# Squared-ReLU attention and two feed-forward layers on one core: the first layer's first token block placed beside the last attention block alone, with GpSimd splitting that block's squares

## The chip, the core and the metric

The kernel runs on one NeuronCore of a Trainium2 chip. The engines are named as in the profile: PE (TensorE, matrix products; PEld is its weight load), DVE (VectorE), ACT (ScalarE), POOL (GpSimd) and SP (SyncE, which only issues transfers here). The metric is the device time of one execution in microseconds; lower is better. Several runs give a median.

## What is computed

```python
def _attn_ref(u, v, z):                      # u, v: 2 x 3008 x 256, z: 2 x 3008 x 64
    scores = (1.0 / S) * np.matmul(z, z.transpose(0, 2, 1))
    attn = np.maximum(scores, 0.0) ** 2
    return (u * np.matmul(attn, v)).astype(np.float32)

def _moe_ref(x, w_in, w_out, a, b):          # x: 6016 x 256, d_ff = 2048
    h = x @ w_in
    P = a[0] + a[1] * h + a[2] * h**2 + a[3] * h**3
    Q = 1.0 + abs(b[0]) * abs(h) + abs(b[1]) * h**2
    return ((P / (Q + 1e-06)) @ w_out).astype(np.float32)

def _moe2_ref(x, w_in, w_out):
    h = x @ w_in
    return (np.maximum(0.01 * h, h) @ w_out).astype(np.float32)

reference = _moe2_ref(_moe_ref(_attn_ref(u, v, z).reshape(6016, 256), ...), ...)
```

## The kernel before

**Numbers in two parts.** Every factor of a product is split into a high part, rounded to fp32r, and a low part, the rest. A product takes three passes on PE: high by high, low by high, high by low. So each tile that ends on PE first needs a rounding (a copy or an activation with an fp32r output) and a subtraction.

**Attention.** Queries are cut into 12 blocks, six for each batch: 512 wide, the sixth (blocks 5 and 11) 448 wide. A block meets 24 key blocks of 128 rows, two at a time, so it has 12 steps (`NPAIR`), numbered through as `t` from 0 to 143 (`NT`). A step is: the scores on PE (`scores_pe`), ReLU and square on ACT (`scores_relu`, `scores_square`), the square's high part and low part on DVE (`square_high`, line 337, and `square_low`, line 343; at some steps ACT writes the high part instead, set `by_act`, line 289), and two steps later the product with V on PE (`av`, line 350). The tiles `r` have three slots, `ph` three, `pl` two.

**Two forms of a block.** Blocks below `SPLIT` (line 84, 10 of them) use 64-row pairs. A score has 64 rows of contraction, so two matmuls of 64 rows stand side by side in the array: six half matmuls a step. In `av` each 128-row product is two half products into two accumulators, 24 a step; at the block's end ACT copies one accumulator (`copy_half`), DVE adds the other (`add_half`) and multiplies by `u` (`gate_halves`). Blocks from `SPLIT` on use 128 rows: the keys' high and low parts are stacked by `stack_keys`, through DRAM, in the steps around `FULL = SPLIT * NPAIR`; a score is four full matmuls, `av` twelve, and `gate` multiplies straight from the accumulators. The other two accumulator banks are then free for `y1`.

**First feed-forward layer.** The 6016 tokens are cut into 12 blocks of 512 (the last 384), the hidden width into eight chunks (`NP`) of 256. Chunk `c` takes: `m1_h`, 12 matmuls into an `h` tile; on ACT `m1_tb`, `m1_s`, `m1_v` (three readings of `h`); on DVE `m1_q` and the two operations of `m1_w`; on ACT `m1_r` (logarithm, then exponential: the reciprocal); on DVE `m1_gh`, `m1_back` and the two of `m1_gl`; then `m1_y`, 12 matmuls into `y1`. Of the seven DVE operations the two of `m1_w` read `h` in PSUM and one tile in SBUF; the other five read two tiles in SBUF. `h` and the score tiles share two PSUM tiles (`big`), used in turn.

**The order of the work** is the order in which the program calls these functions: every engine runs its own list in that order and waits for tiles. From step `m0 = NT + DEPTH - 3 * MERGED` = 119 to the last step, chunks 0 to 8 (`MERGED = NP + 1`) are laid between the steps, one for every three steps:

```python
    m0 = NT + DEPTH - 3 * MERGED
    for t in range(NT + DEPTH):
        c, ph = divmod(t - m0, 3)
```

So the first token block's layer runs beside the last two attention blocks, 10 and 11. Chunk 9's `h` follows at step 144. From chunk 9 on the main loop (lines 853 to 892) pairs each chunk of the first layer with one of the second layer eight chunks back. `tasks`, filled by `at(step, f)`, holds the transfers and small jobs of a step: loads of `u`, of `x1` (`load_x`, `split_x1`), the second layer's weights (`load_w2`), the stores of `xs`. All transfers go through SP, but for a few on ACT at the start and the end.

Of the kernel before, what the change touches and what calls it, by code (L numbers as in the profile page):

```python
# [9 lines left out]
F32 = mybir.dt.float32  # L10
# [7 lines left out]
def f32(ap):  # L18
    return ap.bitcast(F32)
# [3 lines left out]
def squared_relu_attention_moe_moe2(  # L23
# [57 lines left out]

    HALVES = slice(0, 64), slice(64, P)

    SPLIT = NB - 2

    def key_block(i, pr, e):
        if i >= SPLIT or blocks[i][0] == 0 and pr < 4:
# [198 lines left out]
    R, PH, PL = {}, {}, {}  # L286

    SC = {}
    by_act = {0, 1, 2, SPLIT * NPAIR + 2, SPLIT * NPAIR + 3, NB * NPAIR - 2, NB * NPAIR - 1}

    def scores_pe(t):
        i, pr = divmod(t, NPAIR)
# [40 lines left out]

    def scores_square(t):
        act.activation(R[t], R[t], AF.Square)  # L335

    def square_high(t):
        if t in by_act:
# [11 lines left out]
    def av(t, part=None):  # L350
        i, pr = divmod(t, NPAIR)
        b, q0, n = blocks[i]
        ph, pl = PH[t], PL.get(t)
        if part != 0:
            PH.pop(t), PL.pop(t)
        seq = [(0, ph), (1, ph), (0, pl)]
        if i < SPLIT:
            if pr == 0 and part != 1:
                pacc[i] = [acc(k, f"oT{i}_{k}") for k in range(2)]
            steps = [(si, e, j) for si in range(3) for e in range(2) for j in range(2)]  # L360
            if pr == NPAIR - 1:
                steps.sort(key=lambda x: (x[2], (x[:2] == (2, 1)) != x[2]))
            elif pr == 0:
                steps.sort(key=lambda x: x[2] if i else x[0] == 2)
            ops = [(si, e, j, r) for si, e, j in steps for r in range(2)
                   if key_block(i, pr, e) < KB - 1 or si == 1 or si == 2 and r == j]
            last = {(j, r): k for k, (_, _, j, r) in enumerate(ops)}
            for k, (si, e, j, r) in enumerate(ops):
                if part is not None and part != (e == 1 or si == 2):
                    continue  # L370
                h, mv = seq[si]
                kb, rows = key_block(i, pr, e), HALVES[r]
                o = (kb % 4) * D + j * P
                pe.matmul(pacc[i][r][j][:, :n], V[b, kb // 4][rows, h, o : o + P], mv[rows, e, :],  # L374
                          start=pr == 0 and si == 0 and e == 0, stop=pr == NPAIR - 1 and last[j, r] == k)
            if pr == NPAIR - 1:
                at(t + DEPTH + 2, lambda: sp.dma_start(xs[i], uT.pop(i)[:, :, :n]))
            return
        if pr == 0:
            pacc[i] = acc(own_acc(i), f"oT{i}")  # L380
        a = pacc[i]
        for si, (h, mv) in enumerate(seq):
            for e in range(2):
                kb = 2 * pr + e
                if kb == KB - 1 and si == 0:
# [239 lines left out]
    def m1_h(c):  # L625
        i, p = divmod(c, NP)
        T[c] = {"n": tokens[i][1], "h": hidden(f"h1_{c}", 0, p, X1[i], tokens[i][1])}

    def m1_tile(c, key, k, dt=F32):
        T[c][key] = slot(k, f"{key}_{c}", dt)[:, :, : T[c]["n"]]  # L630
        return T[c][key]

    def m1_tb(c):
        if c % 2 and c <= MERGED:
            T[c]["t1"] = extra[1][:, :, : T[c]["n"]]
        else:
            m1_tile(c, "t1", 13 if c % 2 else 2)
        act.activation(T[c]["t1"], T[c]["h"], AF.Abs, scale=b0)  # L638

    def m1_s(c):  # L640
        act.activation(m1_tile(c, "t2", 11 if c == NP else 7 if c > NP and c % 2 else 3), T[c]["h"], AF.Square)  # L641

    def m1_v(c):
        act.activation(m1_tile(c, "t3", 12 if c % 2 else 10), T[c]["h"], AF.Identity, scale=ca[3], bias=ca[2])  # L644
# [98 lines left out]

    TAIL = NC - NP
    MERGED = NP + 1
    m0 = NT + DEPTH - 3 * MERGED
    at(m0 - 5, lambda: load_x(0))
    at(m0 - 3, lambda: split_x1(0))
    at(m0 - 2, lambda: split_x1_low(0))
# [5 lines left out]
    at(20, lambda: act.activation(par[:, 6:7], par[:, 5:6], AF.Abs))  # L755
    for f in tasks.pop(-1):
        f()
    for t in range(NT + DEPTH):
        c, ph = divmod(t - m0, 3)
        c = c if t >= m0 and c < MERGED else None  # L760
        ends = DEPTH < t < FULL and (t - DEPTH + 1) % NPAIR == 0
        waits = ends or DEPTH < t < FULL and (t - DEPTH + 2) % NPAIR == 0
        if t < NT and t != FULL + 1:
            if t == DEPTH:
                av(0, 0)
            if t:
                scores_pe(t)
            if not ends:
                scores_act(t)
            if c == 1 and ph == 2:  # L770
                m1_r(c)
                m1_gh(c)
                m1_back(c)
        if c is not None and ph == 0 and t != FULL - 1:
            m1_h(c)
        if c and c > 1 and ph == 1:
            m1_y(c - 1, (0, 1, 2))
        if t == NT:
            m1_h(MERGED)
        if t >= DEPTH and t != FULL + 1:  # L780
            av(t - DEPTH, 1 if t == DEPTH else None)
        if c == 1 and ph == 1:
            m1_y(0, (0, 1, 2))
        if t == FULL - 1:
            m1_h(c)
        if t == FULL:
            av(t - 1)
            scores_pe(t + 1)
            joined = copy_half(SPLIT - 1, 12)
            add_half(SPLIT - 1, joined)  # L790
            scores_relu(t + 1)
        if ends:
            i = (t - DEPTH) // NPAIR
            joined = copy_half(i, 9)
            scores_act(t)
            add_half(i, joined)
            for f in tasks.pop(t - 1, []):
                f()
        if c == 1 and ph == 0:
            m1_v(c)  # L800
            m1_tb(c)
            m1_s(c)
            m1_w(c)
        if t < NT:
            square_high(t)
        if t == FULL - 1:
            square_low(t)
        if c is not None and c != 1 and ph == 0:
            if c == 0:
                m1_v(c)  # L810
            m1_tb(c)
            m1_s(c)
            if c:
                m1_v(c)
            if c < NP:
                m1_w(c)
            m1_q(c)
        if t == 4:
            tasks[t].pop(0)()
        if t < NT and t != FULL - 1:  # L820
            square_low(t)
        if c == 1 and ph == 0:
            m1_q(c)
        if ends:
            tasks.setdefault(t + 1 + (t + 1 in conv4_at), []).insert(0, lambda i=i, o=joined: gate_halves(i, o))
        if t == FULL:
            gate_halves(SPLIT - 1, joined)
        if c == NP and ph == 0:
            m1_w(c)
        if ends or not waits:  # L830
            for f in tasks.pop(t, []):
                f()
        if c is not None and c != 1 and ph == 1:
            m1_r(c)
            if c == NP:
                split_x2_high(0)
            if c == 0:
                scores_square(FULL + 1)
            m1_gh(c)
            if c == NP:  # L840
                split_x2_low(0)
            m1_back(c)
        if t == NT + 1:
            m1_v(MERGED)
            m1_tb(MERGED)
            m1_s(MERGED)
            m1_w(MERGED)
            m1_q(MERGED)
        if c is not None and ph == 2:
            m1_gl(c)  # L850
    assert not tasks

    for c in range(MERGED, NC):
# [89 lines left out]
```

## Time and profile before

| | |
|---|---|
| median of 3 runs | 1518.52 us (1518.33 to 1521.3) |
| the profiled execution | 1518.12 us, of which its span is 1516.3 us |
| busy in the span | PE 1510.2 us (8546 matmuls), DVE 1346.7, ACT 1111.3, POOL 1.1 |
| granted TensorE clock | 0.9 or more in every slice, mean 1.0 |

The span is the time from the first to the last recorded instruction; the profiled execution's own time holds about 1.8 us around it. Matmuls are pipelined, so the busy time of PE says only that it had work in hand; how long a group of matmuls takes is read from the chain of waits, which follows the last instruction back to what released each step. A duration of an operation on DVE or ACT is a little longer than the distance from one start to the next, since neighbours overlap by some 0.1 us.

### The profile page before, as it was taken

The numbers are of one execution on the slowest core, as the hardware profiler recorded it, in microseconds if no ns is written. First come the engines' busy times: TensorE is split into PE (matmuls) and PEld (weight loads), VectorE is DVE, ScalarE is ACT, GpSimd is POOL, SyncE is SP. The second block draws the span as 40 slices with busy tenths as digits, with TensorE's granted clock in tenths as the row PEclk, the third lists the DMA queues.
The fourth block names the chain that finished last, engine by engine and source line by source line (L and its number), as shares of the span: only waits on it lengthen the run. The fifth ranks groups of instructions, "written<-read, shape, count | busy, mean of one in ns | idle before, by whom it ended". The sixth has DMA issues, their size and how long they took to land.

```text
span 1516.3 us, 21013 instructions
## 1 busy us (share of the span) xinstructions
PE 1510.2 (100%) x8546; PEld 1265.8 (83%) x8546; DVE 1346.7 (89%) x1315; ACT 1111.3 (73%) x1146; POOL 1.1 (0%) x9
## 2 busy tenths in 40 slices
PE   9999999999999999999999999999999999999998
PEld 7888888888788888888888888888888888888888
DVE  8888878888799999999999999999999999999872
ACT  8888878888777866777777676767676767676653
POOL 0000000000000000000000000000000000000000
PEclk9999999999999999999999999999999999999999
DMA  7433426354411520000000000100000000000001
GB/s 177 98 93 95 125 77 144 112 160 138 135 27 35 173 82 14 14 1 14 14 15 14 14 15 0 22 7 14 14 15 14 14 15 0 11 15 1 15 0 25
DMA packets 140351, 74.75 MB, mean 49 GB/s; under 512 B 114528, under 2 KB 124000, under 8 KB 139232
## 3 DMA queue, kind: packets, MB, share of 16 engines
q1 hardware_dynamic: 137584, 72.96, 18.9%
q8 instruction: 67, 1.10, 0.3%
q10 hardware_dynamic: 2672, 0.46, 0.2%
q14 instruction: 28, 0.23, 0.1%
HBM read 46.27 MB, written 21.50 MB: 45 GB/s over the span
## 4 chain that ended last, share of the span: by engine, by line
PE 100%; ACT 0%; DVE 0%; issue 0%
PE h L610 34%; PE y L621 34%; PE oT L374 21%; PE sc L301 5%; PE oT L390 4%; PE sc L308 1%; PE warm L194 0%; ACT r L323 0%; PE zT0q L166 0%; DVE yo L740 0%; ACT sq L210 0%; PE zT0b L166 0%; PE zT0k L166 0%; DVE wt L190 0%
## 5 line engine op out<-in xcount | busy, mean ns | idle before, releaser
L621 PE MATMUL y<-gh,w 128*128 128x512 f32 (+1 forms) x1536 | 373.3, 385 | 0.0
L621 PEld LDWEIGHTS y<-gh,w 128*128 128x128 f32 x1536 | 286.8, 188 | 54.3
L374 PE MATMUL oT<-ph,V 64*128 64x512 f32 (+1 forms) x1880 | 234.0, 384 | 0.0
L374 PEld LDWEIGHTS oT<-ph,V 64*128 64x128 f32 x1880 | 175.9, 184 | 35.5 <-issue 0.4
L621 PE MATMUL y<-gl,w 128*128 128x512 f32 (+1 forms) x768 | 202.2, 385 | 0.0
L638 ACT ACTIVATE t<-h,par 128x1024 f32<-128x1024 f32 (+1 forms) x91 | 100.2, 1101 | 130.4 <-PE h L610 130.4
L697 ACT ACTIVATE gh<-h 128x1024 fp32r<-128x1024 f32 (+1 forms) x96 | 97.0, 1011 | 134.2 <-PE y L621 111.2
L610 PE MATMUL h<-x2h,w 128*128 128x512 f32 (+1 forms) x768 | 186.5, 385 | 0.0
L621 PEld LDWEIGHTS y<-gl,w 128*128 128x128 f32 x768 | 143.5, 188 | 28.0
L610 PEld LDWEIGHTS h<-x2h,w 128*128 128x128 f32 x768 | 143.4, 188 | 27.2
L648 DVE SCALAR_TENSOR_TENSOR t<-t,par,t 128x1024 f32<-128x1024 f32 (+1 forms) x91 | 114.2, 1255 | 31.2 <-ACT t L641 31.2
L657 ACT ACTIVATE t<-t,par 128x1024 f32<-128x1024 f32 (+1 forms) x91 | 103.3, 1135 | 44.1 <-DVE t L648 44.1
L704 DVE TENSOR_TENSOR gl<-g,gh 128x1024 fp32r<-128x1024 f32 (+1 forms) x96 | 115.0, 1198 | 23.2 <-ACT g L699 23.2
L610 PE MATMUL h<-x,w 128*128 128x512 f32 (+1 forms) x576 | 133.5, 380 | 0.0
L374 PE MATMUL oT<-pl,V 64*128 64x512 f32 (+1 forms) x940 | 128.1, 384 | 0.0
L347 DVE TENSOR_TENSOR pl<-r,ph 128x1024 fp32r<-128x1024 f32 (+2 forms) x97 | 115.5, 1192 | 12.2 <-ACT r L335 4.2
L664 DVE SCALAR_TENSOR_TENSOR gh<-t,par,t 128x1024 fp32r<-128x1024 f32 (+1 forms) x91 | 114.6, 1260 | 10.6 <-ACT x2h L588 0.5
L672 DVE SCALAR_TENSOR_TENSOR t<-t,par,t 128x1024 f32<-128x1024 f32 (+1 forms) x96 | 121.1, 1261 | 3.1
L653 DVE SCALAR_TENSOR_TENSOR t<-t,par,h 128x1024 f32<-128x1024 f32 (+1 forms) x96 | 120.8, 1258 | 3.4
L610 PEld LDWEIGHTS h<-x,w 128*128 128x128 f32 x576 | 107.1, 188 | 19.6 <-issue 0.4
L652 DVE TENSOR_TENSOR t<-t,h 128x1024 f32<-128x1024 f32 (+1 forms) x96 | 114.4, 1192 | 7.0 <-ACT t L644 4.1
L673 DVE TENSOR_TENSOR gl<-t,t 128x1024 fp32r<-128x1024 f32 (+1 forms) x91 | 109.3, 1202 | 9.9 <-DVE t L672 0.9
(106 smaller groups left out, 2186.3 us busy)
## 6 DMA issues: line engine op xcount, KB each, us to landing
wraw<-in_moe_w_in_dram SPq DMA_DIRECT2D x16, 512.0 KB, 4.6
wraw<-in_moe_w_out_dram SPq DMA_DIRECT2D x16, 512.0 KB, 4.0
w2s<-wst SPq DMA_DIRECT2D x16, 512.0 KB, 3.5
w<-w2s SPq DMA_DIRECT2D x8, 1024.0 KB, 4.8
out_dram<-yo SPq DMA_DIRECT2D x44, 128.0 KB, 3.2
u<-in_u_dram SPq DMA_DIRECT2D x40, 128.0 KB, 4.6
xs<-u SPq DMA_DIRECT2D x10, 512.0 KB, 2.8
vraw<-in_v_dram SPq DMA_DIRECT2D x9, 512.0 KB, 4.3
```

Source lines behind the costliest of these rows:

```text
L347: dve.tensor_tensor(out=pl[:, part], in0=r[:, part], in1=f32(ph[:, part]), op=ALU.subtract)
L374: pe.matmul(pacc[i][r][j][:, :n], V[b, kb // 4][rows, h, o : o + P], mv[rows, e, :], start=pr == 0 and si == 0 and e == 0, stop=pr == NPAI ...
L610: pe.matmul(h[:, e, :n], w[:, hl, o : o + P], mv[:, k, :n], start=si == 0 and k == 0, stop=si == 2 and k == 1)
L621: pe.matmul(a[j], w[:, hl, o : o + P], mv[:, e, :], start=p == 0 and si == 0 and e == 0, stop=p == NP - 1 and si == 2 and e == 1)
L648: dve.scalar_tensor_tensor(out=d["t2"], in0=d["t2"], scalar=b1, in1=d["t1"], op0=ALU.mult, op1=ALU.add)
L652: dve.tensor_tensor(out=d["t3"], in0=d["t3"], in1=d["h"], op=ALU.mult)
L653: dve.scalar_tensor_tensor(out=d["t3"], in0=d["t3"], scalar=ca[1], in1=d["h"], op0=ALU.add, op1=ALU.mult)
L657: act.activation(d["t1"], d["t2"], AF.Ln, scale=LSH, bias=lnb)
L664: dve.scalar_tensor_tensor(out=m1_tile(c, "gh", 14, F32R), in0=d["t3"], scalar=ca[0], in1=d["t1"], op0=ALU.add, op1=ALU.mult)
L672: dve.scalar_tensor_tensor(out=d["t3"], in0=d["t3"], scalar=ca[0], in1=d["t2"], op0=ALU.add, op1=ALU.subtract)
L673: dve.tensor_tensor(out=m1_tile(c, "gl", 15, F32R), in0=d["t3"], in1=d["t1"], op=ALU.mult)
L704: dve.tensor_tensor(out=d["gl"], in0=d["g"], in1=f32(d["gh"]), op=ALU.subtract)
```

## The change

`SPLIT` becomes `NB - 1` = 11, so block 10 also runs in 64-row pairs, and `FULL` moves from step 120 to step 132; with it move `stack_keys` (steps 124, 128 and 132 instead of 112, 116 and 120) and `m0`, now `FULL - 1` = 131 (with `load_x(0)` and `split_x1(0)` before it). Chunks 0 to 8 stand beside block 11 alone, in a loop over chunks: one attention step for chunks 2, 4, 6 and 7, two for 1, 3, 5 and 8. In all of block 11 the squares are split on GpSimd (`pool_squares`) instead of DVE, and `by_act` loses its steps of blocks 10 and 11. The squares `t2` of odd chunks below 8 get a tile of their own (the query tile of the even blocks, free once block 10 has its last scores).

```diff
-    SPLIT = NB - 2
+    SPLIT = NB - 1
...
-    by_act = {0, 1, 2, SPLIT * NPAIR + 2, SPLIT * NPAIR + 3, NB * NPAIR - 2, NB * NPAIR - 1}
+    by_act = {0, 1, 2}
...
+    def pool_squares(t):
+        n = blocks[t // NPAIR][2]
+        r = R.pop(t)
+        PH[t] = slot(4 + t % 3, f"ph{t}", F32R)[:, :, :n]
+        PL[t] = slot(7 + t % 2, f"pl{t}", F32R)[:, :, :n]
+        pool.tensor_copy(out=PH[t], in_=r)
+        pool.tensor_tensor(out=PL[t], in0=r, in1=f32(PH[t]), op=ALU.subtract)
...
     def m1_s(c):
-        act.activation(m1_tile(c, "t2", 11 if c == NP else 7 if c > NP and c % 2 else 3), T[c]["h"], AF.Square)
+        if c < NP and c % 2:
+            T[c]["t2"] = sb.tile([P, 2, QB], F32, tag="sq", name=f"t2_{c}")[:, :, : T[c]["n"]]
+        else:
+            m1_tile(c, "t2", 11 if c == NP else 7 if c > NP and c % 2 else 3)
+        act.activation(T[c]["t2"], T[c]["h"], AF.Square)
...
-    m0 = NT + DEPTH - 3 * MERGED
+    m0 = FULL - 1
...
+    def squares(t):
+        scores_square(t)
+        pool_squares(t)
+
+    step = FULL
+    for c in range(1, MERGED):
+        two = c % 2 and c < NP - 1
+        if c == 1:
+            scores_pe(step + 2)
+            scores_relu(step + 2)
+            squares(step + 2)
+        m1_h(c)
+        if c == 1:
+            av(step)
+            run_tasks(step + 2)
+            step += 1
+        else:
+            m1_back(c - 1)
+            m1_gl(c - 1)
+        m1_tb(c)
+        m1_s(c)
+        m1_v(c)
+        m1_q(c)
+        m1_w(c)
+        t = step + 2
+        if t < NT:
+            scores_pe(t)
+            scores_relu(t)
+        if c > 1:
+            av(step)
+            run_tasks(step + 2)
+            step += 1
+        m1_r(c)
+        if t < NT:
+            squares(t)
+        m1_y(c - 1, (0, 1, 2))
+        if c == NP:
+            split_x2_high(0)
+        m1_gh(c)
+        if c == NP:
+            split_x2_low(0)
+        if c == 1 or two or c == NP:
+            av(step)
+            run_tasks(step + 2)
+            step += 1
+            if two and c > 1:
+                scores_pe(step + 1)
+                scores_relu(step + 1)
+                squares(step + 1)
+    m1_h(MERGED)
+    m1_back(NP)
+    m1_gl(NP)
```

**The squares leave DVE.** DVE's list before, around chunk 3 in block 10 (`ph` and `pl` are the squares' parts, `t1`, `t2`, `t3`, `extra`, `gh` and `gl` the chunk's tiles):

```order
L341 CAST ph128_5634<-extra_71 128x1024
L652 TENSOR_TENSOR t3_3_5639<-t3_3_5639,h1_3_5609 128x1024
L653 SCALAR_TENSOR_TENSOR t3_3_5639<-t3_3_5639,par_66,h1_3_5609 128x1024
L648 SCALAR_TENSOR_TENSOR t2_3_5637<-t2_3_5637,par_66,extra_71 128x1024
L347 TENSOR_TENSOR pl128_5644<-extra_71,ph128_5634 128x1024
L341 CAST ph129_5678<-r129_5651 128x1024
L347 TENSOR_TENSOR pl129_5680<-r129_5651,ph129_5678 128x1024
L664 SCALAR_TENSOR_TENSOR gh_3_5684<-t3_3_5639,par_66,extra_71 128x1024
L668 SCALAR_TENSOR_TENSOR t2_3_5637<-t2_3_5637,gh_3_5684 128x1024
L341 CAST ph130_5707<-r130_5692 128x1024
```

DVE's list now, around chunks 2 and 3 in block 11:

```order
L660 SCALAR_TENSOR_TENSOR t2_2_5938<-t2_2_5938,par_66,t1_2_5936 128x1024
L664 TENSOR_TENSOR t3_2_5940<-t3_2_5940,h1_2_5919 128x1024
L665 SCALAR_TENSOR_TENSOR t3_2_5940<-t3_2_5940,par_66,h1_2_5919 128x1024
L676 SCALAR_TENSOR_TENSOR gh_2_5985<-t3_2_5940,par_66,t1_2_5936 128x1024
L680 SCALAR_TENSOR_TENSOR t2_2_5938<-t2_2_5938,gh_2_5985 128x1024
L684 SCALAR_TENSOR_TENSOR t3_2_5940<-t3_2_5940,par_66,t2_2_5938 128x1024
L685 TENSOR_TENSOR gl_2_6002<-t3_2_5940,t1_2_5936 128x1024
L660 SCALAR_TENSOR_TENSOR t2_3_6005<-t2_3_6005,par_66,extra_71 128x1024
```

Between one chunk's `t3` with `h` and the next there were up to six operations on squares; now there is none, and four operations in a row (`gh`, `t2`, `t3`, `gl`), with the next chunk's `t2`, read two SBUF tiles each.

**Where the squares become ready.** ACT's list now, for chunk 2 (lines 669 and 670 are the logarithm and the exponential, line 335 the square):

```order
L646 ACTIVATE t1_2_5936<-h1_2_5919,par_66 128x1024
L653 ACTIVATE t2_2_5938<-h1_2_5919 128x1024
L656 ACTIVATE t3_2_5940<-h1_2_5919,par_66 128x1024
L323 ACTIVATE r136_5950<-sc136_5945 128x2x448
L669 ACTIVATE t1_2_5936<-t2_2_5938,par_66 128x1024
L670 ACTIVATE t1_2_5936<-t1_2_5936,par_66 128x1024
L335 ACTIVATE r136_5950<-r136_5950 128x2x448
```

POOL's list at the same place and after it:

```order
L343 TENSOR_TENSOR pl135_5887<-r135_5881,ph135_5886 128x2x448
L342 CAST ph136_5969<-r136_5950 128x2x448
L343 TENSOR_TENSOR pl136_5970<-r136_5950,ph136_5969 128x2x448
L342 CAST ph137_6033<-extra_71 128x2x448
L343 TENSOR_TENSOR pl137_6034<-extra_71,ph137_6033 128x2x448
```

The square of step 136 stands behind chunk 2's exponential, for which the operation on DVE that writes `gh` also waits; POOL's copy and subtraction follow the square.

**The end of block 11 on PE.** Before (the first row of each group of matmuls; `h1_9` is chunk 9's `h`, `h2_0` the second layer's first):

```order
L610 MATMUL h1_8_6195<-x1_1_5940,w0_0_750 128x512 x12
L390 MATMUL oT11_0_5848<-ph141_6145,V1_4_3354 128x448
...
L621 MATMUL y1_0_0_5431<-gh_7_6154,w1_3_2140 128x512
...
L610 MATMUL h1_9_6243<-x1_1_5940,w0_0_750 128x512 x12
L390 MATMUL oT11_0_5848<-ph142_6163,V1_5_3438 128x448
...
L621 MATMUL y1_1_0_6306<-gh_8_6273,w1_0_843 128x512
...
L610 MATMUL h2_0_6316<-x2h0_6270,w2_0_6029 128x512 x8
...
L610 MATMUL h1_10_6343<-x1_1_5940,w0_1_1111 128x512 x12
L621 MATMUL y1_1_0_6306<-gl_8_6304,w1_0_843 128x512
```

And now:

```order
L618 MATMUL h1_8_6375<-x1_1_5964,w0_0_750 128x512 x12
L398 MATMUL oT11_0_5853<-ph142_6293,V1_5_3438 128x448
...
L629 MATMUL y1_0_0_5890<-gh_7_6373,w1_3_2140 128x512
...
L398 MATMUL oT11_0_5853<-ph143_6357,V1_5_3438 128x448
...
L618 MATMUL h1_9_6451<-x1_1_5964,w0_0_750 128x512 x12
L629 MATMUL y1_1_0_6476<-gh_8_6430,w1_0_843 128x512
...
L618 MATMUL h2_0_6486<-x2h0_6427,w2_0_6066 128x512 x8
...
L618 MATMUL h1_10_6513<-x1_1_5964,w0_1_1111 128x512 x12
L629 MATMUL y1_1_0_6476<-gl_8_6466,w1_0_843 128x512
```

Before, `av` of steps 142 and 143 stood between chunk 9's `h` and chunk 8's `y`; now both stand ahead of chunk 9's `h`.

## Rows read from the trace of the kernel before

**Rows 1.** The page: busy time of each engine, and the chain that ended last.

```profile
PE 1510.2 (100%) x8546; PEld 1265.8 (83%) x8546; DVE 1346.7 (89%) x1315; ACT 1111.3 (73%) x1146; POOL 1.1 (0%) x9
...
PE h L610 34%; PE y L621 34%; PE oT L374 21%; PE sc L301 5%; PE oT L390 4%; PE sc L308 1%; PE warm L194 0%; ACT r L323 0%; PE zT0q L166 0%; DVE yo L740 0%; ACT sq L210 0%; PE zT0b L166 0%; PE zT0k L166 0%; DVE wt L190 0%
```

**Rows 2.** Chain of waits, end of block 9, start of 10 (start us, us, what).

```profile
395.44 0.68 PE sc L301 x6
396.12 2.72 PE oT L374 x24
...
402.71 5.01 PE oT L374 x42
...
415.70 0.91 PE sc L308 x4
416.61 2.72 PE oT L390 x12
```

**Rows 3.** Chain of waits, one step of block 11.

```profile
480.04 0.81 PE sc L308 x4
...
483.58 2.43 PE oT L390 x12
```

**Rows 4.** DVE timeline, one chunk of the main loop (start us, us, what).

```profile
709.59 1.28 DVE L648 SCALAR_TENSOR_TENSOR t<-t,par,t 128x1024 f32<-128x1024 f32 x1
710.78 1.21 DVE L652 TENSOR_TENSOR t<-t,h 128x1024 f32<-128x1024 f32 x1
712.03 1.28 DVE L653 SCALAR_TENSOR_TENSOR t<-t,par,h 128x1024 f32<-128x1024 f32 x1
713.45 1.28 DVE L664 SCALAR_TENSOR_TENSOR gh<-t,par,t 128x1024 fp32r<-128x1024 f32 x1
714.76 1.22 DVE L668 SCALAR_TENSOR_TENSOR t<-t,gh 128x1024 f32<-128x1024 f32 x1
716.02 1.28 DVE L672 SCALAR_TENSOR_TENSOR t<-t,par,t 128x1024 f32<-128x1024 f32 x1
717.41 1.23 DVE L673 TENSOR_TENSOR gl<-t,t 128x1024 fp32r<-128x1024 f32 x1
718.55 1.22 DVE L704 TENSOR_TENSOR gl<-g,gh 128x1024 fp32r<-128x1024 f32 x1
```

**Rows 5.** ACT timeline, the second half of the same chunk's reciprocal.

```profile
712.09 1.16 ACT L658 ACTIVATE t<-t,par 128x1024 f32<-128x1024 f32 x1
```

**Rows 6.** DVE timeline, the squares of one step of block 11.

```profile
485.82 0.62 DVE L341 CAST ph<-r 128x896 fp32r<-128x896 f32 x1
486.54 1.09 DVE L347 TENSOR_TENSOR pl<-r,ph 128x896 fp32r<-128x896 f32 x1
```

**Rows 7.** Chain of waits, the end of block 11.

```profile
528.37 2.72 PE h L610 x12
531.09 4.46 PE oT L390 x22
535.55 1.83 PE y L621 x8
537.38 5.44 PE h L610 x24
542.82 2.72 PE y L621 x12
```

**Rows 8.** DVE timeline, the high part of chunk 9.

```profile
540.82 1.28 DVE L664 SCALAR_TENSOR_TENSOR gh<-t,par,extra 128x1024 fp32r<-128x1024 f32 x1
```

**Rows 9.** POOL timeline, whole span.

```profile
0.74 0.20 POOL masks.py:197 MEMSET ident<- 128x128 f32 x1 [0.29 <-POOLq L927]
...
1.03 0.29 POOL masks.py:199 TENSOR_SCALAR_AFFINE_SELECT ident<-ident 128x128 f32<-128x128 f32 x1
406.96 0.31 POOL L534 MEMSET V<- 64x256 f32 x1 [405.63 <-PE oT L374]
```

**Rows 10.** DVE timeline, what ran beside the last of rows 9.

```profile
406.26 1.28 DVE L653 SCALAR_TENSOR_TENSOR t<-t,par,h 128x1024 f32<-128x1024 f32 x1
```

More of the change, by code (lines that the diff above doesn't have):

```diff
@@ L757, in squared_relu_attention_moe_moe2, with run_tasks @@
         f()
-    for t in range(NT + DEPTH):
-        c, ph = divmod(t - m0, 3)
-        c = c if t >= m0 and c < MERGED else None
+    def run_tasks(t):
+        for f in tasks.pop(t, []):
+            f()
+    for t in range(FULL + 2):
         ends = DEPTH < t < FULL and (t - DEPTH + 1) % NPAIR == 0
         waits = ends or DEPTH < t < FULL and (t - DEPTH + 2) % NPAIR == 0
-        if t < NT and t != FULL + 1:
+        if t <= FULL:
             if t == DEPTH:
@@ L769, in squared_relu_attention_moe_moe2 @@
                 scores_act(t)
[L770 to L783, printed above, removed]
+            if t >= DEPTH:
+                av(t - DEPTH, 1 if t == DEPTH else None)
         if t == FULL - 1:
-            m1_h(c)
+            m1_h(0)
         if t == FULL:
@@ L796, in squared_relu_attention_moe_moe2 @@
             add_half(i, joined)
[L797 to L804, printed above, removed]
+            run_tasks(t - 1)
+        if t < FULL:
             square_high(t)
+        elif t == FULL:
+            pool_squares(t)
         if t == FULL - 1:
             square_low(t)
[L808 to L817, printed above, removed]
+            m1_v(0)
+            m1_tb(0)
+            m1_s(0)
+            m1_w(0)
+            m1_q(0)
         if t == 4:
             tasks[t].pop(0)()
-        if t < NT and t != FULL - 1:
+        if t < FULL - 1:
             square_low(t)
-        if c == 1 and ph == 0:
-            m1_q(c)
         if ends:
@@ L827, in squared_relu_attention_moe_moe2 @@
             gate_halves(SPLIT - 1, joined)
-        if c == NP and ph == 0:
-            m1_w(c)
         if ends or not waits:
[L831 to L850, printed above, removed]
+            run_tasks(t)
+        if t == FULL:
+            m1_r(0)
+            scores_square(t + 1)
+            pool_squares(t + 1)
+            m1_gh(0)
+            m1_back(0)
+    m1_gl(0)
+    def squares(t):
+        scores_square(t)
+        pool_squares(t)
+    step = FULL
[46 more added lines that the diff above has]
+    m1_gl(NP)
+    m1_v(MERGED)
+    m1_tb(MERGED)
+    m1_s(MERGED)
+    m1_w(MERGED)
+    m1_q(MERGED)
+    assert step == NT
     assert not tasks
```

## The prediction

> **What bounds the kernel.** First the page: PE is busy for 1510.2 of 1516.3 us, and the chain that ended last is 100% PE [rows 1]. So PE's work is the time, unless another engine makes it wait. DVE is next with 1346.7 us, 89% [rows 1]; it has no room for much more where work on PE is short.
>
> Then the chain of waits, for the price of a step. In block 9 (64-row pairs) a step is 0.68 us of scores and 2.72 of products with V: 3.40. In block 10 (128 rows) it is 0.91 and 2.72: 3.63 [rows 2]. Twelve full matmuls and 24 half ones both take 2.72, so a slot is 0.227 us; pairs save one slot of scores a step. The reader should see pieces that follow each other without a gap. A step of block 11, 448 wide, is 0.81 and 2.43 [rows 3].
>
> Then the DVE timeline for one chunk of the first layer. From `t2` (L648) to the start of the next operation after `gl` (the second layer's, L704) it is 709.59 to 718.55, 8.96 us, nearly without idle. Of these the two that read PSUM (L652, L653) hold 710.78 to 713.45, 2.67 us; the other five, with two tiles in SBUF each, the remaining 6.29, that is 70% [rows 4].
>
> **The change part by part.**
>
> *Block 10 in pairs.* Twelve steps lose a slot: 12 x 0.227 = 2.72 us. The last step's products: a 128-row block leaves out two full matmuls of twelve (22 for the last two steps of block 11 [rows 7]), a paired block six halves of 24 (42 for the last two of block 9 [rows 2]), so one more slot, 0.23. Together **-2.95 us**. ACT and DVE follow a 3.40 us step in block 9 already, and block 10 is now the same. The switch between the two forms happens once, as before, and I cost it at nothing, also the accumulators' copy and sum, which move with it.
>
> *SP.* The three stackings (four transfers each), `load_x(0)` and the first split move twelve steps, past the load of block 10's `u`, still in the same places before `FULL`. The queries of block 11 take four transfers either way. They hide behind PE as they did; uncovered, one such group would cost a few us once. I cost them at nothing.
>
> *DVE's squares.* Block 11's copies and subtractions, 0.62 and 1.09 us a step [rows 6], leave DVE. That is not a gain but the condition of the new place. From `h` of chunk 1 to the `y` of chunk 7 PE has 16 x 2.72 of chunks, eleven products of 2.43 and a last of 2.03 (ten of the twelve matmuls), and nine scores of 0.81 [rows 3, 7]: 79.6 us. DVE has 8 x 8.96 [rows 4] and about 3.6 of jobs of `x1`, `u` and `x2` (three kilocolumn operations of about 1.2, the size of rows 4): 75.3. It fits with 4.3 us left; with the squares, about 20 more, it would not.
>
> *The end of the block.* Before, chunk 9's `h` ended at 531.09 and DVE ended its high part, `gh`, at 540.82 + 1.28 = 542.10, 11.0 us later [rows 7, 8]. PE used the time for the last two products (4.46), then 1.83, 5.44 and a third of 2.72 (the low part of `y` 8) [rows 7]. Now the two products lie ahead of this `h`, and 1.83 + 5.44 + 0.91 = 8.2 us are left. If the chain on ACT and DVE stays as long, PE waits 11.0 - 8.2: **+2.8 us**.
>
> *GpSimd's twelve pairs of operations.* The trace has no copy and no subtraction on POOL. What it has: memsets of 128 and 256 columns, 0.20 and 0.31 us, so 0.86 ns a column and 0.09 fixed; and a select that reads and writes 128 columns in 0.29, so 1.56 ns [rows 9]. For 896 columns that is 0.86 us at the memset's rate, 1.49 at the select's, and 2.9 at twice the select's for the subtraction's two inputs. A pair is therefore between 1.7 and 4.4; I take 3.0, both at the select's rate, the row that also reads and writes. That is 36 us of POOL in 80, so POOL alone holds nobody up.
>
> The open price is what DVE loses meanwhile. The lower bound is nothing; the upper is that a two-tile operation on DVE stands for the whole of a POOL operation. The one row of POOL beside DVE, the memset at 406.96, left the operation at 406.26 at its usual 1.28 us [rows 9, 10], but it reads nothing, and that operation has one operand in PSUM. A price near nothing rests on this row alone. On the other side stands the order: the square is queued on ACT behind the exponential, which ended at 712.09 + 1.16 = 713.25, and it is the exponential that releases `gh`, at 713.45 [rows 4, 5]. The square is one more operation of ACT, about as long; so POOL's pair becomes ready while DVE runs four two-tile operations in a row, and POOL reads the same kind of operand at the same time. I take the upper bound for the share of DVE's time in such operations: 3.0 x 0.70 = 2.1 us a pair, 25.2 for twelve, less the 4.3 that DVE has free: **+20.9 us**. With a pair of 1.7 it is +10.0, with 4.4 +32.7.
>
> What the Trainium skill says of this is a check on the choice. SBUF — State Buffer, section "Who interferes with whom", says that a DVE instruction with two SBUF inputs contends with a GpSimd instruction that reads SBUF, not with one that only writes, and that whoever issues second is blocked for the whole instruction. By that rule the memset of rows 9 could not have shown it, and the sum is the one above; by the row alone it would be 20.9 lower. No run shows yet which holds. GPSIMD Engine Reference, section 3.1, gives 4497 ns for a two-input operation of 2048 columns; an estimate from it is 1.97 us for 896, and with the copy at 1.49 the sum would be about 4 us higher.
>
> **Sum.** 1518.12 - 2.95 + 2.8 + 20.9 = 1538.9 against the profiled execution. The median of the runs is 0.4 higher; I say 1539.
>
> **The rivals.**
>
> *POOL runs beside DVE* and costs it nothing. For it: the memset beside DVE [rows 9, 10]. Then the sum is 1518.12 - 2.95 + 2.8 = 1518.0, with the median 1518.4, not slower: the slot that pairs save goes to the wait behind chunk 9. It decides if DVE's two-tile operations keep their 1.2 to 1.3 us while POOL is at work. 22%.
>
> *The same, and the end of the block finds cover*, because DVE has run ahead there: 1518.4 - 2.8 = 1515.6, a little less if the switch to 128 rows waits less too. Against it: the chain from chunk 9's `h` to `gh` begins with that `h`, however early DVE is. 6%.
>
> *DVE goes first*: POOL comes in only while DVE reads PSUM or idles, and never cuts in between two-tile operations. A chunk's window is 2.67 us [rows 4], and 12 pairs in 9 chunks need 4.0; 1.3 x 9 = 12.0 us of overhang less 4.3 free is +7.7: 1526. PE would then wait for the low parts of the squares in the products with V. Against it: nothing in the rows gives DVE precedence. 12%.
>
> That block 10 gains nothing by pairs is excluded by the even 3.40 us of block 9 [rows 2].
>
> **Numbers.** Forecast 60%: 1539, by the bounds of a pair 1528 to 1551. DVE first 12%: 1526. Beside 22%: 1518.4. Beside and covered 6%: 1515.6 or below. A measurement of this kernel tells about 0.2%, 3.0 us, from no change; so faster 6%, same 22%, slower 72%. The range 1517 to 1549 leaves out the case with cover, a little of the one beside it, and the top of the forecast's own, some 15% in all; the likeliest case alone is 1528 to 1551.
>
> **What would show it.** Right: in block 10 the chain runs at 3.40 us a step. Beside chunks 1 to 8 DVE's `gh`, `t2`, `t3`, `gl` last 2 us and more, or stand idle with no releaser, each time POOL is at work; PE waits in this stretch some 20 us, at the low part of `y` (for `gl`) and at `h` (for DVE's reading of the tile before), and DVE is the releaser. After chunk 9 PE waits again, 2 to 3 us. POOL is busy 20 to 53 us. Wrong: DVE's durations as before and hardly a wait on PE between chunks 1 and 8, which is the first rival; waits of PE for POOL, which is the third; or no wait after chunk 9, which takes my +2.8 away.

## The result, and the profile after

The changed kernel takes **1541.71 us** (median of 4 runs, 1540.55 to 1542.62) against 1518.45 for the kernel before on the same chip: ratio 1.0150 (the two medians alone give 1.0153), 95% interval 1.0138 to 1.0162, so slower. The profiled execution took 1540.55, its span 1538.8, which is 22.5 more than the span before.

The page of the changed kernel, busy time of each engine and the chain that ended last:

```profile
PE 1515.9 (99%) x8710; PEld 1266.2 (82%) x8710; DVE 1359.0 (88%) x1295; ACT 1107.7 (72%) x1145; POOL 53.9 (4%) x33
...
PE 93%; DVE 6%; issue 1%; ACT 0%; DVEq 0%; ACTq 0%
```

Before, the chain was all PE [rows 1]; now DVE has 6% of it. DVE has 20 operations fewer and is busy 12 us longer. The views that follow look for where.

**Block 10.** The chain of waits, last two steps of block 10 and the start of chunk 0's `h` (start, us, what):

```profile
432.18 0.68 PE sc L301 x6
432.86 2.72 PE oT L382 x24
435.58 0.68 PE sc L301 x6
436.26 2.72 PE oT L382 x24
438.98 2.05 PE h L618 x8
```

A step is 3.40 us, as in block 9 before [rows 2], and nothing waits.

**Block 11.** What PE waited for from 400 to 600 us (us in total, times, longest us); the same stretch before has only the like of the last row, 0.2 us on L610:

```profile
PE y L629 <- DVE gl L685: 13.3, 7, 2.3
PE h L618 <- DVE t L665: 2.6, 2, 1.7
PE y L629 <- DVE gh L676: 1.0, 1, 1.0
PE h L618 <- ACT r L323: 0.2, 1, 0.2
```

Seven times PE waited for DVE's `gl`, the last operation of a chunk there. The DVE timeline of one such chunk, from its first reading of `h` to the next chunk's first operation (start, us, what):

```profile
474.48 1.22 DVE L664 TENSOR_TENSOR t<-t,h 128x1024 f32<-128x1024 f32 x1
475.73 1.28 DVE L665 SCALAR_TENSOR_TENSOR t<-t,par,h 128x1024 f32<-128x1024 f32 x1
477.15 1.28 DVE L676 SCALAR_TENSOR_TENSOR gh<-t,par,t 128x1024 fp32r<-128x1024 f32 x1
478.47 1.83 DVE L680 SCALAR_TENSOR_TENSOR t<-t,gh 128x1024 f32<-128x1024 f32 x1
480.34 3.04 DVE L684 SCALAR_TENSOR_TENSOR t<-t,par,t 128x1024 f32<-128x1024 f32 x1
483.48 1.23 DVE L685 TENSOR_TENSOR gl<-t,t 128x1024 fp32r<-128x1024 f32 x1
484.62 1.28 DVE L660 SCALAR_TENSOR_TENSOR t<-t,par,extra 128x1024 f32<-128x1024 f32 x1
```

And POOL's timeline beside it:

```profile
477.84 1.38 POOL L342 CAST ph<-r 128x896 fp32r<-128x896 f32 x1 [6.89 <-ACT r L335]
479.30 2.98 POOL L343 TENSOR_TENSOR pl<-r,ph 128x896 fp32r<-128x896 f32 x1
```

In [rows 4] the operations of L680 and L684 (there L668 and L672) take 1.22 and 1.28 us. Here they take 1.83 and 3.04, with POOL at work. Read side by side, the ends fall in turn: `gh` ends at 478.43, POOL's copy at 479.22; `t2` at 480.30, POOL's subtraction at 482.28; `t3` at 483.38, 1.10 after it. That looks like one whole operation after another. It also says that a duration shown can hold standing time, on both engines. The two operations that read `h` in PSUM take 1.22 and 1.28 as before, but no operation of POOL runs beside them in these rows; experiment 3 has rows where one does.

The sum over the stretch, the DVE groups from 445 to 561 us (busy us, mean ns | idle before):

```profile
L684 DVE SCALAR_TENSOR_TENSOR t<-t,par,t 128x1024 f32<-128x1024 f32 x9 | 24.3, 2704 | 0.3
L680 DVE SCALAR_TENSOR_TENSOR t<-t,gh 128x1024 f32<-128x1024 f32 x9 | 16.2, 1800 | 0.2
L660 DVE SCALAR_TENSOR_TENSOR t<-t,par,t 128x1024 f32<-128x1024 f32 x5 | 8.4, 1670 | 0.0
L660 DVE SCALAR_TENSOR_TENSOR t<-t,par,extra 128x1024 f32<-128x1024 f32 x5 | 8.2, 1650 | 0.0
L685 DVE TENSOR_TENSOR gl<-t,extra 128x1024 fp32r<-128x1024 f32 x4 | 7.2, 1798 | 0.4
L685 DVE TENSOR_TENSOR gl<-t,t 128x1024 fp32r<-128x1024 f32 x5 | 6.7, 1347 | 0.5
L676 DVE SCALAR_TENSOR_TENSOR gh<-t,par,t 128x1024 fp32r<-128x1024 f32 x5 | 6.4, 1284 | 0.6
L676 DVE SCALAR_TENSOR_TENSOR gh<-t,par,extra 128x1024 fp32r<-128x1024 f32 x4 | 5.8, 1451 | 0.4
```

Against the durations of [rows 4], nine of L684 are 12.8 us over, nine of L680 5.2, ten of L660 3.8, nine of L685 2.8, nine of L676 0.7: **25.3 us** in all. And DVE hardly ever idles. The only two rows of its timeline from 445 to 570 us with an idle stretch are these (the bracket is the idle time before):

```profile
445.14 1.22 DVE L664 TENSOR_TENSOR t<-t,h 128x1024 f32<-128x1024 f32 x1 [4.66 <-ACT t L653]
...
563.24 1.28 DVE L676 SCALAR_TENSOR_TENSOR gh<-t,par,extra 128x1024 fp32r<-128x1024 f32 x1 [2.46 <-ACT extra L670]
```

So DVE, not PE, sets the time of block 11. The second row is chunk 9's `gh`; PE's three waits of the end stand round it, in the PE timeline:

```profile
559.73 2.99 PE L618 MATMUL h<-x,w 128*128 128x512 f32 x12 [1.68 <-DVE t L665]
...
564.58 2.11 PE L629 MATMUL y<-gh,w 128*128 128x512 f32 x8 [0.96 <-DVE gh L676]
...
574.30 3.00 PE L618 MATMUL h<-x,w 128*128 128x512 f32 x12 [0.93 <-DVE t L665]
```

### The profile page after: what moved, and what is told of

Read it like the earlier page. It is cut to its first block, busy times and chain, and to the rows that moved or that the text cites. A ratio compares the mean times of both kernels' runs of the same rounds, so it can differ in the third digit from the quotient of the medians.

```text
span 1538.8 us, 21396 instructions
## 1 busy us (share of the span) xinstructions
PE 1515.9 (99%) x8710; PEld 1266.2 (82%) x8710; DVE 1359.0 (88%) x1295; ACT 1107.7 (72%) x1145; POOL 53.9 (4%) x33
## 4 chain that ended last, share of the span: by engine, by line
PE 93%; DVE 6%; issue 1%; ACT 0%; DVEq 0%; ACTq 0%
PE y L629 32%; PE h L618 32%; PE oT L382 23%; PE sc L301 6%; DVE t L684 1%; DVE t L680 1%; DVE t L660 1%; DVE gh L676 1%; DVE t L665 1%; DVE t L664 1%; PE oT L398 0%; PE sc L308 0%; DVE gl L685 0%; PE warm L194 0%; DVE x2l L602 0%
## 5 line engine op out<-in xcount | busy, mean ns | idle before, releaser
L382 PE MATMUL oT<-ph,V 64*128 64x512 f32 (+1 forms) x2068 | 257.7, 384 | 0.0
L382 PEld LDWEIGHTS oT<-ph,V 64*128 64x128 f32 x2068 | 193.8, 184 | 38.9 <-ACT ph L327 0.3
L629 PE MATMUL y<-gl,w 128*128 128x512 f32 (+1 forms) x768 | 204.0, 387 | 13.3 <-DVE gl L685 13.3
L660 DVE SCALAR_TENSOR_TENSOR t<-t,par,t 128x1024 f32<-128x1024 f32 (+1 forms) x91 | 116.2, 1277 | 32.2 <-ACT t L653 32.1
L382 PE MATMUL oT<-pl,V 64*128 64x512 f32 (+1 forms) x1034 | 141.2, 384 | 0.0
L684 DVE SCALAR_TENSOR_TENSOR t<-t,par,t 128x1024 f32<-128x1024 f32 (+1 forms) x96 | 134.0, 1396 | 3.4
L676 DVE SCALAR_TENSOR_TENSOR gh<-t,par,t 128x1024 fp32r<-128x1024 f32 (+1 forms) x91 | 114.6, 1260 | 10.7
L665 DVE SCALAR_TENSOR_TENSOR t<-t,par,h 128x1024 f32<-128x1024 f32 (+1 forms) x96 | 120.9, 1259 | 3.4
L680 DVE SCALAR_TENSOR_TENSOR t<-t,gh 128x1024 f32<-128x1024 f32 (+1 forms) x96 | 120.6, 1256 | 2.9
L664 DVE TENSOR_TENSOR t<-t,h 128x1024 f32<-128x1024 f32 (+1 forms) x96 | 114.4, 1192 | 4.7 <-ACT t L653 4.7
L685 DVE TENSOR_TENSOR gl<-t,t 128x1024 fp32r<-128x1024 f32 (+1 forms) x91 | 110.0, 1209 | 9.4
```

Of the source, the lines that this page charges most:

```text
L629: pe.matmul(a[j], w[:, hl, o : o + P], mv[:, e, :], start=p == 0 and si == 0 and e == 0, stop=p == NP - 1 and si == 2 and e == 1)
L660: dve.scalar_tensor_tensor(out=d["t2"], in0=d["t2"], scalar=b1, in1=d["t1"], op0=ALU.mult, op1=ALU.add)
L664: dve.tensor_tensor(out=d["t3"], in0=d["t3"], in1=d["h"], op=ALU.mult)
L665: dve.scalar_tensor_tensor(out=d["t3"], in0=d["t3"], scalar=ca[1], in1=d["h"], op0=ALU.add, op1=ALU.mult)
L684: dve.scalar_tensor_tensor(out=d["t3"], in0=d["t3"], scalar=ca[0], in1=d["t2"], op0=ALU.add, op1=ALU.subtract)
L685: dve.tensor_tensor(out=m1_tile(c, "gl", 15, F32R), in0=d["t3"], in1=d["t1"], op=ALU.mult)
```

## The experiments

Each kernel is the changed one with the edit shown, timed beside the kernel before.

**1. POOL only writes.** Twelve pairs of memsets stand where the copies and subtractions were.

```diff
-        pool.tensor_copy(out=PH[t], in_=r)
-        pool.tensor_tensor(out=PL[t], in0=r, in1=f32(PH[t]), op=ALU.subtract)
+        pool.memset(f32(PH[t]), 0.0)
+        pool.memset(f32(PL[t]), 0.0)
```

> The changed kernel with POOL's copy and subtraction of each step replaced by two memsets of the same tiles, so that POOL works at the same steps and writes the same tiles but reads nothing (the squares of block 11 are zero). Theory 'one after the other' (a POOL operation that reads SBUF and a DVE operation with two SBUF operands never run together): DVE's L680 and L684 are back at 1.2 to 1.3 us, PE's waits for gl beside chunks 1 to 8 are gone, the wait behind chunk 9 (2 to 4 us) stays, the granted clock is 1.0 throughout; 1517 to 1520 us. Rival 'too tight' (DVE's chain of seven operations cannot follow beside one block alone, whatever POOL does): PE still waits 13 us for gl; 1535 us or more. Rival 'any POOL work' (POOL's writes slow DVE too): L680 and L684 longer by 0.3 to 0.9 us each, 1524 to 1530.

Measured: 1519.88 us, ratio 1.0012 (1.0003 to 1.0022), span 1517.9. The memsets wait for no square, so they run at other moments than the copies and subtractions did, and take 0.85 us each. But some fall beside operations with two SBUF tiles, and these keep their durations; a row of DVE and the row of POOL that lies within it:

```profile
482.15 1.28 DVE L684 SCALAR_TENSOR_TENSOR t<-t,par,t 128x1024 f32<-128x1024 f32 x1
482.38 0.84 POOL L342 MEMSET ph<- 128x896 f32 x1
```

All waits of PE for `gl` are gone, and DVE idles again. Its rows with an idle stretch between the first `h` and chunk 9:

```profile
452.46 1.29 DVE L676 SCALAR_TENSOR_TENSOR gh<-t,par,t 128x1024 fp32r<-128x1024 f32 x1 [0.75 <-ACT t L670]
...
470.60 1.28 DVE L676 SCALAR_TENSOR_TENSOR gh<-t,par,t 128x1024 fp32r<-128x1024 f32 x1 [0.39 <-ACT t L670]
...
487.12 1.29 DVE L660 SCALAR_TENSOR_TENSOR t<-t,par,t 128x1024 f32<-128x1024 f32 x1 [2.36 <-ACT t L653]
...
492.19 1.28 DVE L676 SCALAR_TENSOR_TENSOR gh<-t,par,t 128x1024 fp32r<-128x1024 f32 x1 [1.34 <-ACT t L670]
```

So 4.8 us of DVE are free in this place, and what POOL's copies and subtractions cost beyond memsets is 1538.8 - 1517.9 = 20.9 us of span (21.8 by the medians). 25.3 - 4.8 = 20.5 accounts for it. What is left with memsets in their place is 1.6 us over the span before.

**2. The squares back on DVE, at the same places.**

```diff
-        pool.tensor_copy(out=PH[t], in_=r)
-        pool.tensor_tensor(out=PL[t], in0=r, in1=f32(PH[t]), op=ALU.subtract)
+        dve.tensor_copy(out=PH[t], in_=r)
+        dve.tensor_tensor(out=PL[t], in0=r, in1=f32(PH[t]), op=ALU.subtract)
```

> The changed kernel with the copy and the subtraction issued on DVE at the same places of the program, POOL idle. One after the other: each pair costs DVE about 1.73 us of its own instead of the 2.37 by which POOL makes it wait in the changed kernel, so the time falls by 12 x 0.64 = 8 us at most, less where DVE was waiting anyway: 1533 to 1539. Rival 'POOL relieves DVE' (the loss is in the placement and POOL's help is real): DVE gets 20 us more work with no room, 1555 or more. Too tight: as the changed kernel or worse, 1541 or more.

Measured: 1540.38 us, ratio 1.0143, just above the 1533 to 1539 of the first theory. All durations of the chunks are normal again, but twelve pairs of 1.71 us are added, and the copy waits for ACT's square, 3.8 + 1.6 = 5.4 us in all, which the expectation left out. Three rows of the DVE groups, 445 to 561 us:

```profile
L684 DVE SCALAR_TENSOR_TENSOR t<-t,par,t 128x1024 f32<-128x1024 f32 x9 | 11.6, 1285 | 0.3
...
L342 DVE CAST ph<-r 128x896 fp32r<-128x896 f32 x8 | 5.0, 621 | 3.8 <-ACT r L335 3.8
...
L342 DVE CAST ph<-extra 128x896 fp32r<-128x896 f32 x4 | 2.5, 624 | 1.6 <-ACT extra L335 1.6
```

So in this place a square on POOL (25.3 us for the twelve) costs DVE as much as doing it itself (20.5 of work and these 5.4 of idle time).

**3. The square ahead of the logarithm on ACT**, so that POOL's pair begins before DVE's run of two-tile operations.

```diff
-        m1_r(c)
         if t < NT:
             squares(t)
+        m1_r(c)
```

> The changed kernel with ACT's square of the step put ahead of the logarithm instead of behind the exponential, nothing else; ACT idles about 4 us there for DVE's L660, so the square costs it nothing. POOL's pair then becomes ready before L660 and lies mostly under the two DVE operations that read PSUM (L664, L665). One after the other: DVE loses 0.5 to 1.2 us a pair instead of 2.4 for the eight pairs that move; 1526 to 1533 us. Rival 'any POOL work', or a slowing that does not depend on DVE's operands: the same loss at another place, 1539 to 1543. Too tight: no change.

Measured: 1529.33 us, ratio 1.0070 (1528.28 to 1529.57), as expected. About half of the cost was the place. This trace also shows POOL's own durations where little stood against it:

```profile
495.14 0.94 POOL L342 CAST ph<-r 128x896 fp32r<-128x896 f32 x1 [2.50 <-ACT r L335]
496.16 2.13 POOL L343 TENSOR_TENSOR pl<-r,ph 128x896 fp32r<-128x896 f32 x1
```

0.94 + 2.13 = 3.07 us a pair. The 2.98 us of the changed kernel's subtraction hold some 0.9 of standing behind DVE's L680; none of its twelve is shown under 2.97, so the 2.13 that the expectation of experiment 5 ascribes to it is of this trace. Beside these two operations of POOL, DVE ran its two that read `h` in PSUM, and neither of these was lengthened:

```profile
494.84 1.21 DVE L664 TENSOR_TENSOR t<-t,h 128x1024 f32<-128x1024 f32 x1
496.08 1.28 DVE L665 SCALAR_TENSOR_TENSOR t<-t,par,h 128x1024 f32<-128x1024 f32 x1
```

**4. Chunk 9's `w` and `q` ahead of chunk 8's `gl` on DVE.**

```diff
     m1_h(MERGED)
     m1_back(NP)
-    m1_gl(NP)
...
     m1_q(MERGED)
+    m1_gl(NP)
```

> The changed kernel with chunk 9's t3 and t2 (L664, L665, L660) put ahead of chunk 8's gl (L684, L685), as in the kernel before, so that chunk 9's logarithm and exponential run beside chunk 8's gl. If the wait behind chunk 9 is a chain of DVE and ACT that is too long for the matmuls left: DVE's idle of 2.46 us ahead of chunk 9's gh goes, PE's waits after chunk 9 fall from 3.6 to about 1.5 us; 1538.5 to 1540 us. If it is DVE's lag from POOL that shows there: no change, 1541 to 1542.

Measured: 1541.79 us, ratio 1.0150: no change, the number of the second reading. DVE now stands still ahead of chunk 9's `w`, since ACT has not read that `h` yet:

```profile
559.66 1.22 DVE L664 TENSOR_TENSOR t<-t,h 128x1024 f32<-128x1024 f32 x1 [4.61 <-ACT t L653]
```

The idle stretch before `gh` is gone and a longer one has taken its place. This trace, of the slowest of the four runs (1543.19), is no clean test: just before, from 548 to 552 us, PE ran at a granted clock of 0.50 behind a wait of 3.13 us for chunk 7's `gl`, so chunk 9's `h` came late. In experiment 11, with the same order on DVE and the clock not lowered there, the idle time at this place is 0.20. Why the other three runs gained nothing either is not shown.

**5. A second copy in place of POOL's subtraction.**

```diff
-        pool.tensor_tensor(out=PL[t], in0=r, in1=f32(PH[t]), op=ALU.subtract)
+        pool.tensor_copy(out=PL[t], in_=r)
```

> POOL's subtraction is replaced by a second copy of the square, so the low parts are not the rest (the products with V use other numbers). Alone on POOL a copy took 0.93 us and a subtraction 2.13 in the changed kernel, so POOL's own work falls from 3.06 to 1.86 us a step. One after the other (POOL's and DVE's operations on SBUF take turns as wholes): DVE loses the remainder of the first copy (0.6) and most of a second one (0.7) a step, 1.3 x 12 = 15.6 less the 4.8 us that DVE idles when POOL only writes, so 1519.9 + 10.8 = 1530.7, range 1527 to 1534. If what costs is that POOL comes in at all, twice a step, whatever it does: as the changed kernel, 1539 to 1542. If it is the bytes moved (a copy and a copy against a copy and a subtraction, 4 streams against 5): four fifths of the 20.9, 1536.6.

Measured: 1528.95 us, ratio 1.0068 (1.0053 to 1.0083). DVE's timeline at chunk 2:

```profile
475.12 1.83 DVE L680 SCALAR_TENSOR_TENSOR t<-t,gh 128x1024 f32<-128x1024 f32 x1
476.99 1.83 DVE L684 SCALAR_TENSOR_TENSOR t<-t,par,t 128x1024 f32<-128x1024 f32 x1
```

Each copy adds 0.6 us to the operation that meets it, where the subtraction added 1.75 to L684. The cost follows the length of POOL's operation, not the number of operations: the first theory, at the low side of its range.

**6. As 3, with four of the twelve steps on DVE.**

```diff
+        by = dve if t in (133, 134, 136, 141) else pool
```

> As e3_early (the square ahead of the logarithm), with four of the twelve steps (133, 134, 136 and 141) split on DVE instead of POOL. DVE pays 1.71 us for a step of its own, and lost 13.6 / 12 = 1.1 a step to POOL in e3_early, but more than that at the first steps, where PE waited 2.3 us at 460. One after the other: four steps cost up to 0.6 more each on DVE where POOL was cheap, and up to 1 less where it was dear: 1525 to 1531, likeliest 1528. If early squares on POOL are simply cheaper than anything on DVE: 1532.

Measured: 1532.22 us, ratio 1.0087 (1.0070 to 1.0104). The range missed; the last clause held. In 3 the DVE groups are some 14 us over their usual durations, 1.15 a step; here they are some 8 over, so the four steps gave back some 1.4 each. They were dearer than the mean, as I had expected, but DVE's own pair is 1.71.

**7. As 3, with the high parts on ACT**, so that POOL is left with the subtraction.

```diff
-    by_act = {0, 1, 2}
+    by_act = {0, 1, 2} | set(range(132, 144))
...
-        PH[t] = slot(4 + t % 3, f"ph{t}", F32R)[:, :, :n]
-        pool.tensor_copy(out=PH[t], in_=r)
```

> As e3_early, but ACT writes the high part of all squares of block 11 (a second square of the same ReLU with a rounded output), so POOL is left with the subtraction alone. ACT gains 12 x 0.95 = 11.4 us, of which it has room between the logarithms. One after the other, with POOL's copy (0.93 us) gone: what DVE loses falls from 13.6 to about 9, so 1529.3 - 4.6 = 1524.7, range 1521 to 1528. If ACT's chain sets the time instead (the logarithm stands behind the two squares, 0.95 us later in each of eight chunks, and with it gh): 1529.3 - 4.6 + 7.6 = 1532, and DVE idles before gh with ACT as its releaser.

Measured: 1528.98 us, ratio 1.0070 (1.0055 to 1.0085), between the two. DVE loses about 9.5 us to POOL, as expected, but idles for ACT at three places, 1.11, 1.87 and 1.88 us, one of them:

```profile
478.44 1.28 DVE L674 SCALAR_TENSOR_TENSOR gh<-t,par,t 128x1024 fp32r<-128x1024 f32 x1 [1.87 <-ACT t L668]
```

What POOL gave back, some 5 us, ACT took.

**8. As 7, with the subtraction on DVE.**

```diff
-        pool.tensor_tensor(out=PL[t], in0=r, in1=f32(PH[t]), op=ALU.subtract)
+        dve.tensor_tensor(out=PL[t], in0=r, in1=f32(PH[t]), op=ALU.subtract)
```

> As e7_act_high, with the subtraction on DVE, so POOL is idle in block 11. DVE gains 12 x 1.09 = 13.1 us, less what it idles in e1_fill, 4.8: 1519.9 + 8.3 = 1528.2, range 1525 to 1532; no operation of DVE takes over 1.3 us. If a subtraction on POOL costs DVE less than one of its own (under 1.09 us a step), e7_act_high is the faster of the two; if it costs DVE its whole 2.13 us, this one is, by up to 10 us.

Measured: 1528.67 us, ratio 1.0067 (1.0052 to 1.0082), the same as 7. So block 11 gains nothing by giving POOL, which takes 2.13 us for it, a subtraction of DVE's 1.09.

**9. The cover at the end.** As 1, with the last products with V behind chunk 9's `h`.

```diff
-        if c == 1 or two or c == NP:
+        if c == 1 or two:
             av(step)
...
     m1_h(MERGED)
+    av(step)
+    run_tasks(step + 2)
+    step += 1
```

> As e1_fill (POOL only writes zeros, so block 11's products with V are zero), with the last step's products with V (2.03 us of PE) behind chunk 9's h, as in the kernel before, instead of ahead of it. If the prediction's reason for the wait behind chunk 9 holds (PE lacks cover for a chain that begins with h): 2.0 us of it go, 1519.9 - 2.0 = 1517.9. If the wait is set by DVE's queue instead, which works without idle from chunk 8's gh to chunk 9's q (529.86 to 539.92 in e1_fill, no releaser shown), h comes earlier and nothing else does: 1519.9, within 0.5.

Measured: 1519.79 us, ratio 1.0010 (1.0000 to 1.0019): nothing, as the second reading has it. PE's waits stay:

```profile
PE h L618 <- DVE t L665: 2.1, 2, 1.2
PE y L629 <- DVE gh L676: 1.0, 1, 1.0
```

**10. Cover and order together.** As 9, with the edit of 4.

> As e11_fill_cover, with chunk 9's two operations of w and its q ahead of chunk 8's gl on DVE. If DVE's queue and the cover together set the end: q would end about 537.2 instead of 539.9, gh about 2.4 later as before, w at 536.0 instead of 538.7; PE's 1.35, 0.96 and 0.93 us of waits go, and with restarts 3 to 4 us: 1516 to 1517, so under the kernel before by about the 2.95 us of block 10 less what is left. If the order gives nothing, as in e4_tail: 1519 to 1520.

Measured: 1518.27 us (1517.33 to 1519.57), ratio 0.9996 (0.9986 to 1.0005): 1.5 below 9, which was timed on the same chip, and less than the 3 to 4 expected. Of the three waits one is left, and a short one is new:

```profile
PE h L618 <- DVE t L665: 0.9, 1, 0.9
...
PE y L629 <- DVE gl L685: 0.2, 1, 0.2
```

**11. The same two edits with the squares on POOL, as in 3.**

> As e3_early, with both edits of e9_fill_tail at the end of block 11; all squares are split on POOL. If the contention and the end of the block add up as separate terms: 1529.3 less the 3 to 4 us of the end, 1525.5 to 1526.5. If DVE's queue is the bound there still: DVE's one idle stretch of 2.47 us before gh is filled, no more, 1526.8. If the two waits only change places, as in e4_tail: 1529.

Measured: 1526.99 us, ratio 1.0051 (1.0036 to 1.0066), 2.3 below 3: DVE's idle stretch filled, as the second theory has it. It is the fastest of the versions that do the whole computation, and still slower than the kernel before.

## Why the prediction was right

The forecast of 1539 was 2.7 us low, within its own range of 1528 to 1551. By spans the change is +22.5, where the sum had 20.8. The mechanism is the one that was forecast; the term for the end of the block was too small, and the close fit of the largest term is in part luck.

**Block 10, -2.95: right.** Its steps run at 3.40 instead of 3.63, and its last two steps leave out six halves as in block 9. From the start of block 10's first scores to chunk 0's `h` PE keeps the pace of [rows 2] without a wait.

**GpSimd, +20.9: right in mechanism, and in size with some luck.** By span, experiment 1 gives 20.9. The two inputs also held: 25.2 us lost to twelve pairs against 25.3 measured, 4.3 us of room against 4.8. But the rows allowed a pair anything from 1.7 to 4.4 us. A pair is 3.07 us, where I had taken 3.0, but I had split it evenly; it is 0.94 for the copy and 2.13 for the subtraction. The select of [rows 9] was a good guide for the sum and for neither part. The share of 0.70 stood for a pair that falls anywhere in a chunk, while eight of the twelve pairs followed the exponential into the two-tile operations; there a copy mostly cost 0.6 of its 0.94 us and a subtraction 1.75 of its 2.13. So 0.70 held on average only: the loss depends on which operations the pair meets, as experiment 3 shows with the same pairs at half the price.

Of the signs some came only in part. DVE's `t2`, `t3` and `gl`, with the next chunk's `t2`, are the longer ones; of these `t3` alone lasts over 2 us on average, and `gh` hardly changes. POOL is busy 53.9 us, a little over the 53, with its standing time in it. PE waited 13.3 us for `gl` instead of some 20, and never there for DVE's reading of the tile before an `h`. The rest of what PE lost there is slower work behind the waits: from chunk 1's `h` to the end of chunk 8's it took 20.5 us longer than in experiment 1, of which another 4.7 are the three stretches at half clock of the last section; the other 2.5 are not itemised.

What the Trainium skill states (SBUF — State Buffer, section "Who interferes with whom") agrees with these traces: two-tile operations against a POOL operation that reads, one blocked until the other ends (L684 at 3.04 us beside a subtraction, 1.28 beside a memset), and none with `h` in PSUM (L664 at 1.21 beside a copy, L665 at 1.28 beside a subtraction, experiment 3). The estimate from the Trainium skill's GPSIMD Engine Reference, section 3.1, was 1.97 us for the subtraction; 2.13 was measured. The sum by it was too high all the same, because the copy takes 0.94 and not the 1.49 kept beside it.

**The end of the block, +2.8: too small, and for a reason that was only half right.** Experiment 1 leaves +1.6 of span after -2.95, so the end and small change are worth 4.5. In its trace 3.24 are the three waits of PE at the end (1.35, 0.96, 0.93). The remaining 1.3 I have not accounted for one by one; the first group of matmuls after a wait is somewhat slower (2.98 for an `h` of 2.88). What was wrong in this term is the premise "the chain from chunk 9's `h` to `gh` begins with that `h`", which then lacks cover on PE. Experiment 9 gives the cover back and gains nothing: DVE's queue, from chunk 8's `gh` through its `gl` to chunk 9's `w` and `q`, was the longer path. With the order on DVE changed too (experiment 10) two of the three waits go. The order alone, with the memsets and without the cover, was not run. I had costed chunk 9's `gh` alone, and not the `h` of chunk 10, which waits for `w`, nor that of chunk 11.

**The rivals.** POOL beside DVE for free falls with the rows of L680 and L684 and with experiment 1, which shows what it would have given: 1519.88, close to the 1518.4 worked out. DVE first falls with L684, which stands behind a POOL operation that came between L680 and it. The cover falls with experiment 1: POOL costs nothing there, but PE's waits behind chunk 9 stay.

**Moved costs.** No version that was run beats the kernel before. The 12 x 1.71 = 20.5 us of squares find about 4.8 us of room beside block 11 alone, and each way of placing them costs 8.7 us (11 over 10) to 21.8 (the changed kernel over 1) more than a kernel in which POOL only writes, for a gain of 2.95 in block 10. Whether starting some chunks earlier would make room was not tried.

## What to carry to other kernels

An idle engine is not free help: when GpSimd reads SBUF while DVE runs operations with two SBUF tiles, each waits until the other's operation ends, so price the help at up to GpSimd's duration on DVE, less DVE's own idle time in that stretch; here twelve pairs of 3.07 us, 36.8 in all, cost DVE 25.3 and the kernel 20.9. Look for the place where DVE reads PSUM or waits, and put the help there; here that halved the price. And when the cover of a chain is moved, follow the chain's other start too: the queue of the engine that it runs on.

## What was not expected

After some of its waits PE ran at half its clock for a while. The PE timeline behind the wait at 484.76, and the granted clock there (the third value from a row's end):

```profile
484.76 1.19 PE L629 MATMUL y<-gl,w 128*128 128x512 f32 x4 [2.25 <-DVE gl L685]
485.79 2.85 PE L398 MATMUL oT<-ph,V 128*128 128x448 f32 x8
488.44 1.51 PE L398 MATMUL oT<-pl,V 128*128 128x448 f32 x4
```

```profile
484.70:487.00 2.30, 2.24 (x9) 1.96 (x10) 2.30 (x3) 1.06 (x1) 0.00 (x0) 0.82 0.67 110
487.00:489.00 2.00, 2.00 (x7) 1.80 (x6) 1.83 (x3) 1.97 (x3) 0.00 (x0) 0.50 0.00 0
```

From 487 to 489 us the granted clock is 0.50, so 1.2 of 2.4 GHz; the twelve matmuls took 4.00 us in the chain instead of 2.43 [rows 3]. It happened three times in the changed kernel, some 1.6 us each, behind waits of 2.25, 2.35 and 2.25 us, and not after every wait of that length: behind one of 2.34 at 460 the clock stayed at 1.00. It does not add to the sum here, as far as the trace tells: DVE has no idle stretch there, so PE would have stood longer at the next `gl` instead. In experiment 4 such a stretch delayed an `h` for which DVE then stood still. In experiment 1, whose waits are 1.35 us at most and whose products with V in block 11 are of zeros, the clock is 1.00 in all windows of block 11; in experiment 3, which multiplies all its numbers, it is 1.00 from 465 to 560 us with waits of up to 1.72.
